# Moving the exponential of a linear-attention feature map from ScalarE to a power operation on GpSimd

## The chip, the cores and the metric

The program runs on one core of one Trainium2 chip. The metric is device time in microseconds (us) of one execution. "Span" is the profiled length of one execution, some 2 to 5 us less than its time. A core has TensorE (PE; PEld is its weight load), VectorE (DVE), ScalarE (ACT), GpSimd (POOL) and SyncE (SP), each with its own in-order instruction queue; semaphores connect them.

## The reference, cut to what matters

Two independent blocks whose outputs stand side by side. A is attention with 32 heads over 2048 tokens. B is attention in four segments of 512 tokens, with a memory between the segments: queries and keys pass through the feature map `phi`, and that is where the change acts.

```python
phi = lambda t: jnp.where(t > 0, t + 1.0, jnp.exp(t))
for s in range(4):
    ...                                  # causal softmax attention inside the segment: a_dot
    pq = phi(qs)
    a_mem = (pq @ M) / (pq @ z + 1e-06)  # what the memory gives (einsums in the original)
    o = g * a_mem + (1.0 - g) * a_dot
    pk = phi(ks)
    M = M + pk.T @ vs
    z = z + pk.sum(over tokens)
```

## The kernel before

The kernel is a Python program that simulates the five engines while it emits instructions. Every operation has a `cost`, the estimate of its time in us, and the order of the instructions in each queue follows from these estimates. On the chip the order is fixed; semaphores only make an engine wait.

```python
class Recorder:
    def op(self, eng, fn, r=(), w=(), cost=0.1, mode="F"):
        ...                              # dependencies from the keys read (r) and written (w)
        t = self.free[eng]
        for d in op.deps:
            t = max(t, d.end + LAT)
        op.end = t + cost                # the plan's idea of when this is done
        self.free[eng] = op.end
        self.all.append(op)              # this order is the engine's queue
```

A group of four heads of one segment is prepared by `b_prep`: 32 groups in all. KQ holds keys and queries of one group, 128 partitions x (2 tiles of 512 columns). The first and the last segment need only one of the two tiles (`nk` is 1), the middle segments both. phi(t) is computed as max(t, 0) + min(exp(t), 1):

```python
    def b_prep(self, n):
        ...
        ex = R.op("ACT", lambda e: e.activation(self.E[:, k0:k1, :], KQ[:, k0:k1, :], ACTF.Exp),
                  r=[("KQB", b, k) for k in range(k0, k1)], w=["E"], cost=0.2 + 0.43 * nk)
        R.op("DVE", lambda e: e.tensor_scalar(PH[:, k0:k1, :], KQ[:, k0:k1, :], 0.0, None, ALU.max), ...)
        yield ("t", ex.end)              # go on when the plan says that the exponential is done
        R.op("DVE", lambda e: e.tensor_scalar(self.E[:, k0:k1, :], self.E[:, k0:k1, :], 1.0, None, ALU.min), ...)
        ph = R.op("DVE", lambda e: e.tensor_tensor(PH[:, k0:k1, :], PH[:, k0:k1, :], self.E[:, k0:k1, :], ALU.add), ...)
        ...                              # memory terms: Mb and Zb on GpSimd, den and amem on VectorE
```

Two other pieces matter. The exponentials of the scores of A and B (`PT<-ps`) are ScalarE's main work. The weighted values of all units gather in a single PSUM bank that VectorE must copy away before TensorE can fill it again:

```python
    def emit_pv(self, u, st, part):
        ...                              # TensorE: values and row sums into the bank OLB
        if end:
            R.op("DVE", lambda e: e.tensor_copy(self.OL[x][:, :], self.ps[:, OLB, :]), r=[("ps", OLB)], w=[("OL", x)], cost=0.66)

    def finish(self, u):                 # VectorE: two reciprocals, then operations with two SBUF inputs
        ...
            R.op("DVE", lambda e: e.scalar_tensor_tensor(L, L, 1.0, rec, ALU.mult, ALU.add, accum_out=...), ...)
            op = R.op("DVE", lambda e: e.tensor_tensor(self.OTA[:, u.g, q0:q0 + QC], O, rec, ALU.mult), ...)
```

In the traces, `OL<-ps` is that copy, `OL<-OL,SQ` and `OTA<-OL,SQ` are the two-input operations of `finish`, and GpSimd's `PT<-PT` (affine select) is the causal mask of B.

Of the kernel before, what the change touches and what calls it, by code (L numbers as in the profile page):

```python
# [6 lines left out]
ACTF = mybir.ActivationFunctionType  # L7
ALU = mybir.AluOpType
AX = mybir.AxisListType
BF, F32 = dt.bfloat16, dt.float32  # L10

P = 128
# [223 lines left out]
class Kernel:  # L236
# [66 lines left out]
    def sb(self, name, shape, dtype=BF):  # L303
        return self.es.enter_context(self.nc.sbuf_tensor(name, shape, dtype))

    def alloc(self):
        sb = self.sb
        self.ps = self.es.enter_context(self.nc.psum_tensor("ps", [P, 8, 512], F32))
        self.psb = self.ps.bitcast(BF)
        self.xA = sb("xA", [P, NI, S])  # L310
        self.OTA = sb("OTA", [P, NG, S])
        self.WoB = sb("WoB", [P, NG, D])
        self.WA = [sb(f"WA{k}", [P, NI, P]) for k in range(3)]
        self.KA = [sb(f"KA{i}", [P, S]) for i in range(2)]
        self.QA = [sb(f"QA{i}", [P, S]) for i in range(2)]
        self.VA = [sb(f"VA{i}", [P, NT, P]) for i in range(2)]
        self.xB = [sb(f"xB{i}", [P, NI, 512]) for i in range(2)]
        self.OTB = [sb(f"OTB{i}", [P, NG, 512]) for i in range(2)]
        self.WB = [sb(f"WB{k}", [P, NI, P]) for k in range(3)]
        self.PT = sb("PT", [P, RING, 512])  # L320
        self.KQB = [sb(f"KQB{i}", [P, 2, 512]) for i in range(2)]
        self.VB = [sb(f"VB{i}", [P, 4, 144]) for i in range(2)]
        self.E = sb("E", [P, 2, 512])
        self.PH = [sb(f"PH{i}", [P, 2, 512]) for i in range(2)]
        self.PKt = sb("PKt", [P, 4, P])
        self.VT = [sb(f"VT{i}", [P, 512]) for i in range(2)]
        self.SQB = [sb(f"SQB{i}", [P, 512]) for i in range(2)]
        self.VTB = self.SQB[1]
        self.SQ = [sb(f"SQ{i}", [P, 512]) for i in range(2)]
        self.Mf = sb("Mf", [P, NG, 129], F32)  # L330
        self.Mb = sb("Mb", [P, P])
        self.Zb = sb("Zb", [P, P])
        self.OL = [sb(f"OL{i}", [P, 2 * QC], F32) for i in range(2)]

        self.rec = [t.bitcast(F32) for t in self.SQ]
        self.rng = self.SQB[0].bitcast(F32)
        self.flag = sb("flag", [P, 2], dt.int32)
        self.den = sb("den", [P, 512], F32)
        self.amem = [sb(f"amem{i}", [P, 512], F32) for i in range(2)]
        self.outsb = [sb(f"outsb{i}", [P, D]) for i in range(2)]  # L340
        self.cbA = [sb(f"cbA{i}", [P, 12], F32) for i in range(2)]
        self.cbB = [sb(f"cbB{i}", [P, 4], F32) for i in range(2)]
        self.beta = sb("beta", [P, 32])
        self.gcol = sb("gcol", [P, 2, 8], F32)
        self.ident = sb("ident", [P, P])
        self.ones32 = sb("ones32", [P, 32])
        self.blk32 = sb("blk32", [P, 32])
        self.ones = sb("ones", [P, P])
        self.diag = [sb(f"diag{i}", [P, P]) for i in range(2)]
        self.maskbd = sb("maskbd", [P, P], F32)  # L350


    def load_WA(self, k, g):
# [72 lines left out]
    def constants(self):  # L426
        R = self.R

        def pool(f, w, r=()):
            R.op("POOL", f, r=r, w=w, cost=0.3)  # L430
        R.op("DVE", lambda e: e.memset(self.PT[:, RING - 1, :], 1.0), w=[("PT", RING - 1)], cost=0.2)
        nb = sum(len(b) for b in SLOTS)
        for b in range(nb):
            R.op("DVE", lambda e, b=b: e.memset(self.ps[:, b, :], 0.0), w=[("ps", b)], cost=0.4)

        R.op("ACT", lambda e: e.activation(self.gcol[:, 0, :], self.PT[:, RING - 1, 0:8], ACTF.Exp), r=[("PT", RING - 1)], w=["gcol"], cost=1.5)
        pool(lambda e: e.memset(self.blk32[:, :], 1.0), ["blk32"])
        pool(lambda e: e.affine_select(self.blk32[:, :], self.blk32[:, :], pattern=[[-32, 4], [0, 8]],
                                       compare_op=ALU.is_ge, fill=0.0, base=0, channel_multiplier=1), ["blk32"])
        pool(lambda e: e.affine_select(self.blk32[:, :], self.blk32[:, :], pattern=[[32, 4], [0, 8]],  # L440
                                       compare_op=ALU.is_ge, fill=0.0, base=31, channel_multiplier=-1), ["blk32"])
        pool(lambda e: e.memset(self.ones[:, :], 1.0), ["ones"])
        pool(lambda e: e.memset(self.ident[:, :], 0.0), ["ident"])
        pool(lambda e: e.affine_select(self.ident[:, :], self.ident[:, :], pattern=[[-1, P]],
                                       compare_op=ALU.not_equal, fill=1.0, base=0, channel_multiplier=1), ["ident"])
        for i in range(2):
            pool(lambda e, i=i: e.memset(self.VB[i][:, :, :], 1.0), [("VB", i)])
        pool(lambda e: e.memset(self.maskbd[:, :], 1.0), ["maskbd"])
        pool(lambda e: e.affine_select(self.maskbd[:, :], self.maskbd[:, :], pattern=[[-32, 4], [0, 32]],
                                       compare_op=ALU.is_ge, fill=0.0, base=0, channel_multiplier=1), ["maskbd"])  # L450
        pool(lambda e: e.affine_select(self.maskbd[:, :], self.maskbd[:, :], pattern=[[32, 4], [0, 32]],
                                       compare_op=ALU.is_ge, fill=0.0, base=31, channel_multiplier=-1), ["maskbd"])
        pool(lambda e: e.memset(self.Mf[:, :, :], 0.0), [("Mf", g) for g in range(NG)])
# [342 lines left out]
    def b_prep(self, n):  # L796
        R = self.R
        s, g = n // 8, n % 8
        b = n % 2
        xb = s % len(self.xB)  # L800
        nxt = n + 1
        KQ, VB, PH = self.KQB[b], self.VB[b], self.PH[b]
# [8 lines left out]
        if self.shifted:  # L811
# [3 lines left out]
            for k in range(2):  # L815
                op = R.op("DVE", lambda e, k=k: e.tensor_tensor(self.SQB[k][:, :], KQ[:, k, :], KQ[:, k, :], ALU.mult),
                          r=[("KQB", b, k)], w=[("SQB", k)], cost=0.36)
# [21 lines left out]
        k0, k1 = (0, 1) if s == 0 else ((1, 2) if s == 3 else (0, 2))  # L839
        nk = k1 - k0  # L840
        if n > 0:
            yield ("ev", ("memB", n - 1))
        yield ("t", R.lastw[("KQB", b, 1)].end)
        ex = R.op("ACT", lambda e: e.activation(self.E[:, k0:k1, :], KQ[:, k0:k1, :], ACTF.Exp),  # L844
                  r=[("KQB", b, k) for k in range(k0, k1)], w=["E"], cost=0.2 + 0.43 * nk)
        R.op("DVE", lambda e: e.tensor_scalar(PH[:, k0:k1, :], KQ[:, k0:k1, :], 0.0, None, ALU.max),
             r=[("KQB", b, k) for k in range(k0, k1)], w=[("PH", b)], cost=0.28 * nk)
        yield ("t", ex.end)
        R.op("DVE", lambda e: e.tensor_scalar(self.E[:, k0:k1, :], self.E[:, k0:k1, :], 1.0, None, ALU.min),
             r=["E"], w=["E"], cost=0.28 * nk)  # L850
        ph = R.op("DVE", lambda e: e.tensor_tensor(PH[:, k0:k1, :], PH[:, k0:k1, :], self.E[:, k0:k1, :], ALU.add),
                  r=["E", ("PH", b)], w=[("PH", b)], cost=0.36 * nk)
        yield ("dve",)
        if s > 0:

            R.op("POOL", lambda e: e.tensor_tensor(self.Mb[:, :], self.Mf[:, g, 0:P], self.maskbd[:, :], ALU.mult),
                 r=[("Mf", g), "maskbd"], w=["Mb"], cost=0.3)
            zb = R.op("POOL", lambda e: e.tensor_scalar(self.Zb[:, :], self.maskbd[:, :], self.Mf[:, g, P:P + 1], None, ALU.mult),
                      r=[("Mf", g), "maskbd"], w=["Zb"], cost=0.3)
# [3 lines left out]
                 r=["Zb", ("PH", b)], w=[("ps", bank)], cost=0.3)  # L863
            op = R.op("DVE", lambda e, bank=bank: e.tensor_scalar(self.den[:, :], self.ps[:, bank, :], 1e-6, None, ALU.add),  # L864
                      r=[("ps", bank)], w=["den"], cost=0.66)
            self.bank_release(bank, op)
            for q in range(4):
# [6 lines left out]
                 r=["Mb", ("PH", b)], w=[("ps", bank)], cost=0.3)  # L874
# [4 lines left out]
                      r=[("ps", bank), "den", "gcol"], w=[("amem", b, 0), ("amem", b, 1)], cost=0.66)  # L879
            self.bank_release(bank, op)  # L880
            self.events.add(("amem", n))
        if s < 3:
# [7 lines left out]
            def fm(e, bank=bank):  # L890
                for tl in range(4):
# [4 lines left out]
                      r=[("ps", bank), ("Mf", g)], w=[("Mf", g)], cost=0.3)  # L896
# [274 lines left out]
```

## Time and profile before

| | before |
|---|---|
| time, median of 3 runs | 1200.93 us (1200.85 to 1205.26) |
| ScalarE, TensorE, VectorE, GpSimd busy | 1125, 1043, 803, 117 us |
| exponentials of phi on ScalarE | 16 x 665 ns and 16 x 1092 ns |

Line numbers (L532) are those of the kernel at hand and shift by a few lines from one kernel to the next. The page of the kernel before: busy time per engine (share of the span, instructions), then the chain of work that ended last by engine and by line.

```profile
PE 1042.5 (87%) x16699; PEld 481.9 (40%) x16927; DVE 803.4 (67%) x1363; ACT 1125.4 (94%) x1256; POOL 116.5 (10%) x192
...
ACT 47%; PE 40%; DVE 10%; issue 3%; DMA 1%; SPq 0%; DVEq 0%
```

ScalarE is nearly always busy, and the chain alternates between it and TensorE. The groups of instructions, by line and shape (count | total us, mean ns | idle time before them):

```profile
L532 ACT ACTIVATE PT<-ps 128x1024 bf16<-128x1024 f32 x1088 | 1012.9, 1061 | 31.5 <-PE ps L506 29.5
...
L844 ACT ACTIVATE E<-KQB 128x1024 bf16<-128x1024 bf16 x16 | 17.5, 1092 | 0.0
...
L844 ACT ACTIVATE E<-KQB 128x512 bf16<-128x512 bf16 x16 | 10.6, 665 | 0.0
```

The second and third line are what the change takes from ScalarE: 17.5 + 10.6 = 28.1 us. The view of tile E says who waits for its result (us in total, times):

```profile
who waited for it (us, times):
  DVE E L849: 2.8, 5
```

VectorE waits for E only 2.8 us in the whole run: the plan places the minimum (line 849) where E is ready.

### The profile page before, as it was taken

To read this page: it belongs to the slowest core of one execution; us is meant where nothing else is said; L and a number is where in the kernel's file an instruction comes from. 1 tells how busy PE (TensorE), PEld (TensorE's weight loads), DVE (VectorE), ACT (ScalarE), POOL (GpSimd) and SP (SyncE) were. 2 spreads that over 40 slices of the span, in tenths; PEclk is the share of its full clock that TensorE was granted. 3 is DMA by queue.
4 is the path that set the end of the run, shared out by engine and by line. 5 is a ranking of instruction groups with operands and counts; after the bars stand their busy time and mean duration, and the time that the engine had idled before them with its cause. 6 is when DMAs were issued, how large, how long until landed. Compare 5 with 4: busy or idle time off the path is not lost.

```text
span 1198.7 us, 37080 instructions
## 1 busy us (share of the span) xinstructions
PE 1042.5 (87%) x16699; PEld 481.9 (40%) x16927; DVE 803.4 (67%) x1363; ACT 1125.4 (94%) x1256; POOL 116.5 (10%) x192
## 2 busy tenths in 40 slices
PE   8998889999888888888988897978989887789996
PEld 4343444444344333334444443434444343334442
DVE  5248567576786687866777768677777668774443
ACT  3799999999999999999999999999999999999990
POOL 1001001010101020200111102010110102010000
PEclk9999999999999979899999998989999898989998
DMA  5461132243111122141212121211221110401101
GB/s 172 100 162 38 32 86 59 60 89 76 42 37 41 39 48 54 31 82 32 68 38 45 46 50 37 60 24 37 49 66 41 32 42 15 102 20 37 37 37 56
DMA packets 198344, 66.45 MB, mean 55 GB/s; under 512 B 189986, under 2 KB 189986, under 8 KB 198178
## 3 DMA queue, kind: packets, MB, share of 16 engines
q1 hardware_dynamic: 198178, 63.99, 23.1%
q8 instruction: 135, 2.21, 0.8%
q14 instruction: 31, 0.25, 0.1%
HBM read 39.85 MB, written 8.39 MB: 40 GB/s over the span
## 4 chain that ended last, share of the span: by engine, by line
ACT 47%; PE 40%; DVE 10%; issue 3%; DMA 1%; SPq 0%; DVEq 0%
ACT PT L532 46%; PE ps L674 21%; PE ps L581 9%; PE ps L506 8%; DVE SQ L604 2%; DVE OL L591 2%; DVE den L870 1%; ACT E L844 1%; DVE OL L608 1%; DVE amem L877 1%; DMA OTA<-in_A_x_dram 1%; DVE OTA L612 0%; DVE den L864 0%; DVE outsb L919 0%; DMA out_dram<-outsb 0%
## 5 line engine op out<-in xcount | busy, mean ns | idle before, releaser
L532 ACT ACTIVATE PT<-ps 128x1024 bf16<-128x1024 f32 (+1 forms) x1216 | 1102.4, 1039 | 32.4 <-PE ps L506 30.1
L581 PE MATMUL ps<-PT,ones 128*32 128x256 bf16 (+1 forms) x4864 | 295.6, 275 | 0.0
L581 PE MATMUL ps<-PT,VA 128*32 128x256 bf16 x4096 | 251.8, 277 | 20.9 <-ACT PT L532 15.0
L506 PE MATMUL ps<-QA,KA 32*128 32x256 bf16 x4096 | 213.2, 277 | 39.6 <-ACT PT L532 31.3
L604 DVE RECIPROCAL SQ<-OL 128x128 f32<-128x128 f32 x256 | 242.8, 948 | 4.9
L674 PE MATMUL ps<-xB,WB 128*128 128x512 bf16 x684 | 179.2, 383 | 21.2 <-issue 11.6
L674 PE MATMUL ps<-xA,WA 128*128 128x512 bf16 x695 | 181.6, 387 | 16.5 <-issue 8.7
L506 PEld LDWEIGHTS ps<-QA,KA 32*128 32x128 bf16 x4096 | 62.7, 92 | 224.8 <-ACT PT L532 201.0
L581 PEld LDWEIGHTS ps<-PT,VA 128*32 128x32 bf16 x4096 | 108.2, 95 | 111.3 <-issue 65.3
L552 POOL TENSOR_SCALAR_AFFINE_SELECT PT<-PT 128x512 bf16<-128x512 bf16 x128 | 85.9, 672 | 666.3 <-ACT PT L532 661.2
L581 PEld LDWEIGHTS ps<-PT,ones 128*32 128x32 bf16 x4864 | 131.6, 98 | 2.5
L591 DVE COPY OL<-ps 128x512 f32<-128x512 f32 x128 | 85.6, 669 | 30.3 <-PE ps L581 29.4
L674 PEld LDWEIGHTS ps<-xA,WA 128*128 128x128 bf16 x768 | 63.2, 99 | 93.9 <-issue 27.9
L674 PEld LDWEIGHTS ps<-xB,WB 128*128 128x128 bf16 x768 | 61.8, 98 | 95.2 <-issue 45.3
L919 DVE CAST outsb<-ps 128x512 bf16<-128x512 f32 x64 | 43.5, 680 | 76.2 <-PE ps L674 71.4
L870 DVE RECIPROCAL den<-den 128x128 f32<-128x128 f32 x96 | 91.2, 950 | 2.3
L684 DVE CAST KQB<-ps 128x512 bf16<-128x512 f32 x64 | 43.7, 683 | 57.8 <-PE ps L674 57.4
L674 PE MATMUL ps<-xA,OTA 128*128 128x512 bf16 x236 | 59.5, 391 | 8.5 <-DVE OTA L612 3.7
L674 PE MATMUL ps<-WoB,OTB 128*128 128x512 bf16 x232 | 59.7, 380 | 6.6 <-issue 2.9
L581 PE MATMUL ps<-PT,VB 128*32 128x256 bf16 (+1 forms) x768 | 50.8, 282 | 15.3 <-DVE OL L591 12.0
L608 DVE SCALAR_TENSOR_TENSOR OL<-OL,SQ 128x256 f32<-128x256 f32 x128 | 58.2, 455 | 2.7
L684 DVE CAST VT<-ps 128x512 bf16<-128x512 f32 x32 | 22.0, 687 | 47.7 <-PE ps L674 44.3
(64 smaller groups left out, 490.9 us busy)
## 6 DMA issues: line engine op xcount, KB each, us to landing
WB<-in_B_wk_dram SPq DMA_DIRECT2D x32, 256.0 KB, 3.0
WB<-in_B_wq_dram SPq DMA_DIRECT2D x32, 256.0 KB, 2.9
WB<-in_B_wv_dram SPq DMA_DIRECT2D x32, 256.0 KB, 3.2
out_dram<-outsb SPq DMA_DIRECT2D x32, 256.0 KB, 2.0
WA<-in_A_wqkv_dram SPq DMA_DIRECT2D x24, 256.0 KB, 3.8
OTA<-in_A_x_dram SPq DMA_DIRECT2D x16, 256.0 KB, 5.6
WoB<-in_B_wo_dram SPq DMA_DIRECT2D x1, 2048.0 KB, 10.2
xA<-in_A_wo_dram SPq DMA_DIRECT2D x1, 2048.0 KB, 10.3
```

Source lines behind the costliest of these rows:

```text
L506: ins = e.matmul(o, l, r, start=True, stop=True)
L532: op = R.op("ACT", lambda e: e.activation(self.PT[:, s0:s0 + n, 0:width], self.ps[:, banks[0]:banks[0] + n, 0:width], ACTF.Exp, bias=cb, s ...
L552: mo = R.op("POOL", lambda e, ap=ap, pat=pat: e.affine_select(ap, ap, pattern=pat, compare_op=ALU.is_ge, fill=0.0, base=0, channel_multipl ...
L581: ins = e.matmul(o, l, r, start=start, stop=end, skip_group_check=True)
L591: R.op("DVE", lambda e: e.tensor_copy(self.OL[x][:, :], self.ps[:, OLB, :]), r=[("ps", OLB)], w=[("OL", x)], cost=0.66)
L604: R.op("DVE", lambda e, cs=cs: e.reciprocal(rec[:, cs], L[:, cs]), r=[ko], w=[k], cost=0.93)
L608: R.op("DVE", lambda e: e.scalar_tensor_tensor(L, L, 1.0, rec, ALU.mult, ALU.add, accum_out=self.rng[:, u.seq:u.seq + 1]), r=[k, ko], w=[k ...
L674: ins = e.matmul(o, l, rh, start=a, stop=z)
L684: op = self.R.op("DVE", lambda e: e.tensor_copy(dst, self.ps[:, bank, :]), r=[("ps", bank)], w=[dkey], cost=0.66)
L844: ex = R.op("ACT", lambda e: e.activation(self.E[:, k0:k1, :], KQ[:, k0:k1, :], ACTF.Exp), r=[("KQB", b, k) for k in range(k0, k1)], w=["E ...
L870: R.op("DVE", lambda e, cs=cs: e.reciprocal(self.den[:, cs], self.den[:, cs]), r=["den"], w=["den"], cost=0.9)
L919: op = R.op("DVE", lambda e, ns=ns, bank=bank, ob=ob: e.tensor_copy(self.outsb[ob][:, ns], self.ps[:, bank, :]), r=[("ps", bank)], w=[("ou ...
```

## The change: its intent, and the diff

ScalarE is the busiest engine and GpSimd the idlest. The exponential of phi is to become `pow(e, t)` on GpSimd, so that ScalarE gets 28 us of its queue back. The plan is told 0.2 + 1.5 us for one tile of 512 columns and 3.2 us for two.

```diff
+        self.base = sb("base", [P, 1], F32)
...
+        pool(lambda e: e.memset(self.base[:, :], 2.718281828459045), ["base"])
...
-        ex = R.op("ACT", lambda e: e.activation(self.E[:, k0:k1, :], KQ[:, k0:k1, :], ACTF.Exp),
-                  r=[("KQB", b, k) for k in range(k0, k1)], w=["E"], cost=0.2 + 0.43 * nk)
+        ex = R.op("POOL", lambda e: e.tensor_tensor(self.E[:, k0:k1, :].rearrange("p k n -> p (k n)"),
+                                                    self.base[:, 0:1].to_broadcast([P, 512 * nk]),
+                                                    KQ[:, k0:k1, :].rearrange("p k n -> p (k n)"), ALU.pow),
+                  r=[("KQB", b, k) for k in range(k0, k1)] + ["base"], w=["E"], cost=0.2 + 1.5 * nk)
```

## The prediction

> **What bounds the kernel now.** The engine table gives ScalarE 1125 us busy of a 1199 us span (94%), TensorE 1043 (87%), VectorE 803 (67%), GpSimd 117 (10%). The chain that ended last is ScalarE for 47%, nearly all of it the score exponentials (1216 instructions, 1102 us), and TensorE for 40%. ScalarE is about 99% busy from 70 to 1050 us, but it is fed by an in-order TensorE queue that is 86 to 90% busy in the same windows.
>
> **What the change removes.** 32 exponentials of phi from ScalarE: 16 of 128x512 (665 ns) and 16 of 128x1024 (1092 ns), 28.1 us in all by the groups of instructions, 2.3% of the span. Since TensorE is near its limit too, I expect half to two thirds of it at most: 12 to 18 us.
>
> **What it adds.** 32 two-input pow operations on GpSimd, of the same sizes. The change's own costs are 1.7 and 3.2 us. From the trace, the ordinary two-input multiply on GpSimd of 128x128 took 407 to 622 ns, so by size alone (an estimate, some 100 ns of it fixed) about 1.3 and 2.5 us for 512 and 1024 columns. The Trainium skill (GPSIMD Engine Reference, section 3.1) says that these operations run as software loops, with about 2.6 cycles per element for a two-input add; no run here shows a pow. A pow in software needs a logarithm and an exponential, so my central guess is three to four times the add: about 5 us for 512 columns and 9 us for 1024.
>
> **How much is on the critical path.** The static schedule of every engine was made with 1.7 and 3.2 us. VectorE's minimum on E stands in its in-order queue at the place where the model had pow finished. Each microsecond that pow is late stops VectorE there (now 2.8 us in all), and behind it the copy of the single PV bank (OL<-ps), which the next PV needs; the ring of probability tiles keeps ScalarE going only for some microseconds. GpSimd's causal masks queue behind pow too. With 5 and 9 us the excess is about 3.3 and 5.8 us; taking about 3 us of slack each time, 16 x 0.5 + 16 x 3 = 56 us, plus some for VectorE operations with two SBUF inputs: the skill (SBUF — State Buffer, who interferes with whom) calls the pair that VectorE and GpSimd share an exclusive lock held for the whole instruction. No run here shows that yet. Less the gain of about 15 us: plus 45 to 50 us.
>
> **Prediction.** 1250 us, 8 in 10 between 1188 and 1550. If pow takes what the change assumes, about 1190 to 1200. Faster by over 2%: 0.05; within 2%: 0.33; slower by over 2%: 0.62.
>
> **What would show each step right or wrong.** ScalarE's busy time must fall by 28 us to about 1097. The group of pow on GpSimd gives its mean by shape: over 4 us for 512 columns is my central case, near 1.7 is the case "same". VectorE's wait at the minimum on E should grow from 2.8 to over 60 us, and TensorE's for OL<-ps and ScalarE's for scores with it. VectorE's two-input operations get longer under a pow if the lock matters.
>
> **What would make it wrong.** Pow being as quick as modelled, or far slower (tens of microseconds each, then 1500 us and more); slack in VectorE's queue larger than 3 us; or the reshuffled greedy schedule winning or losing a per cent by itself.

## The result, and the profile after

The changed kernel takes 4933.02 us (median of 4 runs, 4930.09 to 4938.39) against 1200.89 us before: 4.11 times as long, 95% interval 4.09 to 4.12. Ratios in this document are the mean time of one kernel's fast runs over that of the other's in the same rounds, so they are not quite the ratio of the medians quoted.

The page after, the same lines as above: busy time, then the chain that ended last.

```profile
PE 1109.4 (22%) x16703; PEld 504.3 (10%) x16927; DVE 3083.7 (63%) x1363; ACT 1110.1 (23%) x1224; POOL 4040.5 (82%) x225
...
DVE 45%; POOL 37%; PE 10%; ACT 7%; issue 1%; DMA 0%; SPq 0%; another core or an unknown queue 0%; DVEq 0%
```

ScalarE and TensorE do the same work as before, apart from the 32 exponentials, spread over four times the span. (TensorE's busy time is 67 us higher, at a mean granted clock of 0.61 against 0.97; beside 3732 us this is small, and no run here isolates it.) GpSimd went from 117 to 4041 us. VectorE seems to have 2280 us more work, although it runs the same 1363 instructions; as shown below, most of it is something else than work. GpSimd's groups by shape show where the time starts:

```profile
L846 POOL TENSOR_TENSOR E<-base,KQB 128x1024 bf16<-128x1024 f32 x16 | 2612.1, 163254 | 167.6 <-DVE KQB L686 167.5
L846 POOL TENSOR_TENSOR E<-base,KQB 128x512 bf16<-128x512 f32 x16 | 1311.2, 81950 | 230.2 <-DVE KQB L686 230.2
```

One pow of 512 columns takes 81.95 us, one of 1024 takes 163.25 us; the plan said 1.7 and 3.2, and the prediction 5 and 9. Together the 32 take 3923 us, and the kernel became 3732 us longer.

Three of VectorE's groups in the kernel before (all shapes of a line together; line 846 there is the maximum, line 850 after):

```profile
L608 DVE SCALAR_TENSOR_TENSOR OL<-OL,SQ 128x256 f32<-128x256 f32 x128 | 58.2, 455 | 2.7
...
L612 DVE TENSOR_TENSOR OTA<-OL,SQ 128x256 bf16<-128x256 f32 x64 | 31.5, 492 | 2.2
...
L846 DVE TENSOR_SCALAR PH<-KQB 128x512 bf16<-128x512 bf16 (+1 forms) x32 | 11.5, 360 | 0.0
```

The same three after, and the minimum on E with the idle time before it:

```profile
L850 DVE TENSOR_SCALAR PH<-KQB 128x512 bf16<-128x512 bf16 (+1 forms) x32 | 1432.0, 44749 | 0.0
L610 DVE SCALAR_TENSOR_TENSOR OL<-OL,SQ 128x256 f32<-128x256 f32 x128 | 752.2, 5876 | 2.7
...
L614 DVE TENSOR_TENSOR OTA<-OL,SQ 128x256 bf16<-128x256 f32 x64 | 193.4, 3022 | 2.2
...
L853 DVE TENSOR_SCALAR E<-E 128x512 bf16<-128x512 bf16 (+1 forms) x32 | 18.6, 580 | 1437.7 <-POOL E L846 1437.7
```

So VectorE stood still in two ways: 1438 us waiting for E, and, inside instructions that normally take under half a microsecond, (1432.0 - 11.5) + (752.2 - 58.2) + (193.4 - 31.5) = 2276 us. The two add up to 3714 us, nearly all of the growth of 3732 us. Behind VectorE, everything stands. The timeline of the changed kernel around one pow (start us, duration us):

```profile
1433.36 163.24 POOL L846 TENSOR_TENSOR E<-base,KQB 128x1024 bf16<-128x1024 f32 x1 [0.19 <-DVE KQB L686]
...
1436.39 160.49 DVE L850 TENSOR_SCALAR PH<-KQB 128x1024 bf16<-128x1024 bf16 x1
1596.80 0.67 DVE L593 COPY OL<-ps 128x512 f32<-128x512 f32 x1
...
1597.53 0.40 PE L583 MATMUL ps<-PT,VA 128*32 128x256 bf16 x4 [159.63 <-DVE OL L593]
...
1600.45 1.94 ACT L534 ACTIVATE PT<-ps 128x1024 bf16<-128x1024 f32 x2 [160.45 <-PE ps L508]
```

VectorE's maximum, a 0.4 us instruction, starts 3 us after pow and ends 0.3 us after it. The copy of the PV bank comes next, then TensorE resumes after 160 us, then ScalarE after 160 us.

### The profile page after: what moved, and what is told of

Same layout as the page of the kernel before. It is cut to its first block, busy times and chain, and to the rows that moved or that the text cites. A ratio compares the mean times of both kernels' runs of the same rounds, so it can differ in the third digit from the quotient of the medians.

```text
span 4932.7 us, 37082 instructions
## 1 busy us (share of the span) xinstructions
PE 1109.4 (22%) x16703; PEld 504.3 (10%) x16927; DVE 3083.7 (63%) x1363; ACT 1110.1 (23%) x1224; POOL 4040.5 (82%) x225
## 4 chain that ended last, share of the span: by engine, by line
DVE 45%; POOL 37%; PE 10%; ACT 7%; issue 1%; DMA 0%; SPq 0%; another core or an unknown queue 0%; DVEq 0%
POOL E L846 37%; DVE PH L850 29%; DVE OL L610 9%; ACT PT L534 7%; PE ps L676 5%; DVE OTA L614 3%; PE ps L583 3%; PE ps L508 2%; DVE SQ L606 1%; DVE OL L593 1%; DVE PH L855 0%; DVE E L853 0%; DVE KQB L686 0%; DMA out_dram<-outsb 0%; DVE SQB L686 0%
## 5 line engine op out<-in xcount | busy, mean ns | idle before, releaser
L846 POOL TENSOR_TENSOR E<-base,KQB 128x512 bf16<-128x512 f32 (+1 forms) x32 | 3923.3, 122602 | 397.7 <-DVE KQB L686 397.7
L850 DVE TENSOR_SCALAR PH<-KQB 128x512 bf16<-128x512 bf16 (+1 forms) x32 | 1432.0, 44749 | 0.0
L853 DVE TENSOR_SCALAR E<-E 128x512 bf16<-128x512 bf16 (+1 forms) x32 | 18.6, 580 | 1437.7 <-POOL E L846 1437.7
L610 DVE SCALAR_TENSOR_TENSOR OL<-OL,SQ 128x256 f32<-128x256 f32 x128 | 752.2, 5876 | 2.7
L583 PE MATMUL ps<-PT,VA 128*32 128x256 bf16 x4096 | 270.1, 292 | 870.7 <-DVE OL L593 780.8
L583 PE MATMUL ps<-PT,ones 128*32 128x256 bf16 (+1 forms) x4864 | 318.9, 291 | 0.0
L508 PE MATMUL ps<-QA,KA 32*128 32x256 bf16 x4096 | 223.7, 289 | 262.5 <-DVE PH L855 150.3
L676 PE MATMUL ps<-xA,WA 128*128 128x512 bf16 x696 | 191.9, 405 | 233.3 <-DVE Mf L899 147.6
L614 DVE TENSOR_TENSOR OTA<-OL,SQ 128x256 bf16<-128x256 f32 x64 | 193.4, 3022 | 2.2
L583 PEld LDWEIGHTS ps<-PT,VB 128*32 128x32 bf16 x768 | 22.9, 105 | 1110.1 <-POOL PT L554 396.9
```

What stands on the lines that cost most here:

```text
L508: ins = e.matmul(o, l, r, start=True, stop=True)
L583: ins = e.matmul(o, l, r, start=start, stop=end, skip_group_check=True)
L676: ins = e.matmul(o, l, rh, start=a, stop=z)
L846: ex = R.op("POOL", lambda e: e.tensor_tensor(self.E[:, k0:k1, :].rearrange("p k n -> p (k n)"), self.base[:, 0:1].to_broadcast([P, 512 * ...
```

## The experiments

Theory 1: pow itself is slow on GpSimd, per column, whatever it is given; everything else follows from that. Theory 1 leaves open how a slow pow stops the other engines: through those who wait for its result (theory D, dependency), or by keeping VectorE out of SBUF ports that, by this theory, both share (theory L, lock). The rival to theory 1: a producer of E on GpSimd is costly by its place, whatever the operation.

### 1. Pow by itself: m1_bench

The kernel before with a row of GpSimd instructions after all its work, each waiting for the one before (core of the edit; `b2` is 2.0 in place of e, `W` holds ones):

```diff
+        pool(lambda e: e.tensor_tensor(X[:, 0:512], be(P, 512), K[:, 0:512], ALU.mult))
+        pool(lambda e: e.tensor_tensor(X[:, 0:1024], be(P, 1024), K[:, 0:1024], ALU.mult))
+        pool(lambda e: e.tensor_tensor(X[:, 0:128], be(P, 128), K[:, 0:128], ALU.pow))
+        pool(lambda e: e.tensor_tensor(X[0:16, 0:127], be(16, 127), K[0:16, 0:127], ALU.pow))
+        pool(lambda e: e.tensor_tensor(X[0:1, 0:122], be(1, 122), K[0:1, 0:122], ALU.pow))
+        pool(lambda e: e.tensor_tensor(X[:, 0:126], b2(P, 126), K[:, 0:126], ALU.pow))
+        pool(lambda e: e.tensor_tensor(X[:, 0:125], be(P, 125), W[:, 0:125], ALU.pow))
+        pool(lambda e: e.tensor_tensor(X[:, 0:64], be(P, 64), K[:, 0:64], ALU.pow))
```

> The kernel before, and after all its work a row of GpSimd instructions that nobody but the next one waits for, each timed by the profile. Theory 1 (the software of pow itself is slow, per element): multiply 128x512 about 1.3 us and 128x1024 about 2.5 us, pow 128x128 about 21 us (0.65 us + 128 x 0.159 us, from the trace after), base 2 in place of e and exponents of 1.0 in place of data the same 0.159 us per column. Rival (pow is slow only for this data or this base): the variants with base 2 or exponent 1.0 differ by a factor. If the software goes lane by lane, one partition takes a small part of what 16 take; if it works on all lanes at once, 1, 16 and 128 partitions take the same per column.

Measured, timeline of GpSimd at the end of that run, in the order of the edit:

```profile
1194.89 1.04 POOL L657 TENSOR_TENSOR E<-base,KQB 128x512 bf16<-128x512 f32 x1 [129.81 <-DVE E L653]
1196.01 1.89 POOL L658 TENSOR_TENSOR E<-base,KQB 128x1024 bf16<-128x1024 f32 x1
1197.98 20.75 POOL L659 TENSOR_TENSOR E<-base,KQB 128x128 bf16<-128x128 f32 x1
1218.81 20.56 POOL L660 TENSOR_TENSOR E<-base,KQB 16x127 bf16<-16x127 f32 x1
1239.45 19.76 POOL L661 TENSOR_TENSOR E<-base,KQB 1x122 bf16<-1x122 f32 x1
1259.29 20.41 POOL L662 TENSOR_TENSOR E<-base,KQB 128x126 bf16<-128x126 f32 x1
1279.77 20.25 POOL L663 TENSOR_TENSOR E<-base,ones 128x125 bf16<-128x125 f32 x1
1300.10 10.52 POOL L664 TENSOR_TENSOR E<-base,KQB 128x64 bf16<-128x64 f32 x1
```

A multiply costs (1.89 - 1.04) / 512 = 1.7 ns per column, a pow (20.75 - 10.52) / 64 = 160 ns: some 95 times as much. All pow lines give 162 to 164 ns when divided by their columns: base 2 or e, data or ones, 128 partitions, 16 or one. So the cost belongs to the operation and its number of columns, it was the same for both bases and for both kinds of exponent tried, and using fewer partitions saved nothing. Exponents of other sizes were not tried: the keys here are close to 0 (the reference's inputs give them a standard deviation of about 0.0025, an estimate: 32 x 0.05 x 0.05 / 32). The Trainium skill (Perfetto Trace Analysis, section GPSIMD Engine Instruction) advises to time GpSimd by the spacing of starts and not by the reported duration; here both agree (1197.98 to 1218.81 is 20.83 us). The run itself, a single one whose state is unknown, took 1318.62 us, which is its added tail. Why a pow takes this long, no run shows.

### 2. The same change with multiply: m2_mult

```diff
-                                                    KQ[:, k0:k1, :].rearrange("p k n -> p (k n)"), ALU.pow),
+                                                    KQ[:, k0:k1, :].rearrange("p k n -> p (k n)"), ALU.mult),
```

> The changed kernel with multiply in place of pow, everything else the same (wrong result on purpose). Theory 1 (pow's own duration is the whole loss): 1185 to 1205 us, ScalarE busy about 1097 us, GpSimd about 60 us more than before. Rival (a producer of E on GpSimd is costly by its place: handover, in-order queue, the pair of ports shared with VectorE): 1250 us or more.

Measured: 1187.78 us against 1202.87, ratio 0.987 (0.985 to 0.989), the result wrong as intended. The page's busy line:

```profile
PE 1037.5 (87%) x16703; PEld 486.6 (41%) x16927; DVE 801.2 (68%) x1363; ACT 1101.7 (93%) x1224; POOL 161.2 (14%) x225
```

The rival falls. With an operation as quick as the plan believes, the move is worth 15 us, and VectorE no longer waits for E at all. This is the whole prize of the idea.

### 3. Pow as long as the prediction had assumed: m3_dose

Pow acts on 28 columns, or on 27 of each of two tiles; the rest of E keeps the constant 1 from the start.

```diff
+        pool(lambda e: e.memset(self.E[:, :, :], 1.0), ["E"])
...
+        nc = 28 if nk == 1 else 27
+        ex = R.op("POOL", lambda e: e.tensor_tensor(self.E[:, k0:k1, 0:nc],
+                                                    self.base[:, 0:1].unsqueeze(1).to_broadcast([P, nk, nc]),
+                                                    KQ[:, k0:k1, 0:nc], ALU.pow),
```

> The changed kernel with pow on only 28 columns (one 512-column tile) or 2 x 27 columns (two tiles), so that pow takes about 5.1 and 9.2 us, the durations that the prediction assumed; the rest of E keeps a constant (wrong result on purpose). The prediction's model of the critical path (3 us slack, excess counts): 1250 us. Rival, every microsecond of pow stops VectorE and with it everything: up to 1190 + 229 = about 1420 us. Rival, the queues absorb it: 1210 us or less.

Measured: 1240.46 us against 1202.87, ratio 1.030 (1.028 to 1.032). Pow took 4.82 and 8.99 us on average. The view of tile E:

```profile
who waited for it (us, times):
  DVE E L855: 50.7, 18
```

Against m2_mult the run is 52.7 us longer, and VectorE's wait for E, absent in m2_mult, is 50.7 us. So the prediction's model of the critical path was sound: it said 56 us for pows of 5 and 9 us (the same sum gives 47 us for 4.82 and 8.99), and "everything stops for all of every pow" or "the queues absorb it" would have missed. The result passed the comparison with the reference although most of E was the constant 1: the arguments of phi are so small in this input (about 0.0025, the estimate above) that exp(t) is nearly 1. A passed comparison is therefore weak evidence about this exponential here.

### 4. A pow that nobody waits for: m4_lone, then n1_lone512 and n2_lone576

Does pow stop VectorE without being waited for? In the trace of the changed kernel, long VectorE instructions occur under pows of 1024 columns alone, never under those of 512. First try, with one pow of 512 columns at the end of B:

```diff
+                    if u.kn == 31 and u.half == 0 and k == len(todo):
+                        R.op("POOL", lambda e: e.tensor_tensor(self.E[:, 0, :], self.base[:, 0:1].to_broadcast([P, 512]),
+                                                               self.KQB[1][:, 1, :], ALU.pow),
+                             r=[("KQB", 1, 1), "base"], w=["E"], cost=0.1)
```

> The kernel before, with one pow of 128x512 (about 82 us) on GpSimd after its last causal mask, writing E when nobody reads it any more. Theory D (the loss comes only through engines that wait for E or for GpSimd's queue): unchanged, 1200 +- 3 us. Theory L (VectorE instructions with two SBUF inputs or in a fast mode can't run while GpSimd holds the shared ports): VectorE stands still in one instruction for most of 82 us while attention of A still goes on, and the time is 1265 to 1283 us.

Measured: 1281.33 us against 1202.87, ratio 1.065. It looks like theory L, but the run was badly made: the condition held twice, and a mask came between the two pows. GpSimd's timeline:

```profile
1064.16 81.95 POOL L560 TENSOR_TENSOR E<-base,KQB 128x512 bf16<-128x512 f32 x1
1146.08 0.65 POOL L554 TENSOR_SCALAR_AFFINE_SELECT PT<-PT 128x512 bf16<-128x512 bf16 x1
```

TensorE waited 77.8 us for that mask, so the run shows only the cost of a mask queued behind a pow in GpSimd's in-order queue. The second try puts exactly one pow behind the very last mask, once with 512 and once with 576 columns:

```diff
+                    if u.kn == 31 and it.scored + n == len(it.slots) and k == n:
+                        flat = lambda t: t[:, :, :].rearrange("p k n -> p (k n)")[:, 0:576]
+                        R.op("POOL", lambda e: e.tensor_tensor(flat(self.E), self.base[:, 0:1].to_broadcast([P, 576]),
+                                                               flat(self.KQB[1]), ALU.pow),
+                             r=[("KQB", 1, 0), ("KQB", 1, 1), "base"], w=["E"], cost=0.1)
```

> The kernel before with exactly one pow of 128x512 (82 us) on GpSimd behind the very last causal mask; nobody reads what it writes. The trace after showed that VectorE instructions with two tensor inputs or in a fast mode were held up only under pows of 1024 columns. Theory D (a pow costs only through those who wait for its result or its queue): 1202 +- 4 us. Theory L (any pow holds the shared ports all the time): 1265 us or more.

> The same with 576 columns (about 92 us). If a pow of more than 512 columns is worked off in pieces of 512 and keeps VectorE's two-input instructions out until its last input is read, VectorE stands for about 75 us in one instruction under it and the time is 1265 to 1285 us. If the length alone counts and nobody waits: 1202 +- 4 us, as with 512.

Measured: with 512 columns 1201.42 us against 1200.54, ratio 1.000 (0.998 to 1.002); with 576 columns 1284.52 us, ratio 1.069 (1.067 to 1.072). The timelines of GpSimd and VectorE under these two pows, first with 512 columns:

```profile
1064.94 82.22 POOL L561 TENSOR_TENSOR E<-base,KQB 128x512 bf16<-128x512 f32 x1
...
1065.39 1.14 DVE L638 SCALAR_TENSOR_TENSOR OL<-OL,gcol,SQ 128x256 f32<-128x256 f32 x1
1066.56 0.42 DVE L640 TENSOR_TENSOR OTB<-OL,amem 128x256 bf16<-128x256 f32 x1
```

and with 576 columns:

```profile
1066.78 92.48 POOL L561 TENSOR_TENSOR E<-base,KQB 128x576 bf16<-128x576 f32 x1
...
1067.23 81.70 DVE L638 SCALAR_TENSOR_TENSOR OL<-OL,gcol,SQ 128x256 f32<-128x256 f32 x1
```

An 82 us pow of 512 columns held a two-input VectorE instruction for some 0.7 us at its start and then let VectorE work freely; it cost nothing. A pow only 10 us longer held the same instruction until 82.2 us after the pow's start, the time that 512 columns take, and cost 84 us. So a pow of more than 512 columns can stop VectorE though nobody waits for it.

The trace of the changed kernel shows two kinds of hold-up under its 16 pows of 1024 columns. All 11 of the `OL<-OL,SQ` and `OTA<-OL,SQ` instructions (two inputs in SBUF) that started in the first half of such a pow ended 82.6 to 82.7 us after the pow's start. The single-input maximum (line 850, 0.43 us for 1024 columns in the kernel before) fell under 13 of these pows, and ended each time 0.3 us after the pow's end, whether it had started in the first half or the second. Reciprocals and copies out of PSUM kept their usual length. Under pows of 512 columns the maximum ran as usual.

The Trainium skill (SBUF — State Buffer, section Who interferes with whom) says that a VectorE instruction with two SBUF inputs contends with a GpSimd instruction that reads SBUF, and that one in a 2-port performance mode contends with GpSimd, the first to issue having the shared pair for the whole instruction. The contention is here; for two-input instructions neither run shows a hold for the whole of the pow. That the input is read piece by piece and the two-input instructions are released when the last piece is read is my reading of these times, not something a record names. It does not say why the maximum stands longer; that stays open.

### 5. Does that hold-up cost time in the changed kernel: n3_split

Every pow of 1024 columns becomes two of 512; nothing else changes.

```diff
-        ex = R.op("POOL", lambda e: e.tensor_tensor(self.E[:, k0:k1, :].rearrange("p k n -> p (k n)"),
-        ...
+        for k in range(k0, k1):
+            ex = R.op("POOL", lambda e, k=k: e.tensor_tensor(self.E[:, k, :], self.base[:, 0:1].to_broadcast([P, 512]),
+                                                             KQ[:, k, :], ALU.pow),
+                      r=[("KQB", b, k), "base"], w=[("E", k)], cost=0.1 + 1.5)
```

> The changed kernel with each pow of 1024 columns as two pows of 512, so that VectorE is not held up in the ports any more (if the trace after was read rightly). Theory D (VectorE, in order, would stand at the minimum on E just as long): 4930 us within 1%, with VectorE's wait at that minimum up from 1438 to about 3700 us and its 75 to 160 us long instructions gone. Theory L (the port hold-up costs time of its own): under 4700 us.

Measured: 4868.02 us. Against the changed kernel's 4933.02 us (from another chip job, each beside its own runs of the kernel before: 4.054 and 4.106 times) that is 1.3% less. The page's busy line, and the list of waits:

```profile
PE 1091.5 (22%) x16703; PEld 499.6 (10%) x16927; DVE 808.7 (17%) x1363; ACT 1108.3 (23%) x1224; POOL 4048.4 (83%) x241
...
DVE E L853 <- POOL E L847: 3651.0, 32, 159.6
```

VectorE's blown-up busy time is gone, 3084 to 809 us (under these pows the maximum of 1024 columns took 0.42 us in the median), and its wait for E rose from 1438 to 3651 us. The time hardly moved. Theory D holds: the port hold-up was real, but it only changed in which instruction VectorE stood. At most the last 1.3% (the expectation said within 1%) belongs to the hold-up and to the different plan of this run; the runs don't part these two.

### 6. A plan that knows what pow takes: n4_truecost and p1_planned

The first takes n3_split with `cost=82.0` for a tile. The second takes m3_dose with `cost=0.9 + 4.15 * nk` (5.05 and 9.2 us) in place of 1.7 and 3.2.

> As the run before it, but the schedule is told what a pow really takes (82 us for 512 columns in place of 1.6). GpSimd's own work is about 3925 + 117 us, so nothing under about 4040 us is to be had. If the loss above that is the schedule's wrong idea of pow: 4050 to 4250 us, with ScalarE's work under the pows. If each pow is in a chain that can't be overlapped anyway: over 4700 us.

Measured (two runs): 4420.93 us, ratio 3.68. This lies between the two expectations. ScalarE's other work did move under the pows (the chain that ended last is 90% GpSimd), so some 450 us of the loss was the plan's wrong idea. Of the 380 us above the 4040 us of GpSimd's own work, GpSimd spent 325 us waiting for the next group's keys and queries:

```profile
POOL E L847 <- DVE KQB L686: 324.5, 23, 64.4
```

> As the run with 28 and 2 x 27 columns (4.8 and 9.0 us a pow, 1240 us), but the schedule is told 5.05 and 9.2 us in place of 1.7 and 3.2. If its 52 us over the multiply version come from VectorE standing at E earlier than the data is there, a true plan takes them away: 1185 to 1200 us, with VectorE's wait for E near zero. If a longer producer costs by itself (longer chain per head group, masks queued behind it): 1215 us or more.

Measured: 1190.69 us against 1202.34, ratio 0.990 (0.989 to 0.992). The view of tile E:

```profile
who waited for it (us, times):
  POOL E L848: 4.0, 2
  DVE E L855: 1.8, 2
```

The same instructions of 4.8 and 9 us that cost 52.7 us with a wrong plan cost 2.9 us (1190.69 - 1187.78, from two jobs) with a right one. In this statically ordered kernel an error in the cost number was a cost by itself.

### 7. A real exponential of cheap GpSimd instructions: q1_squares and q2_squares2

If about 9 us per group are free, an exponential of additions and multiplications might win. The formula (1/2 + v*v/512)^16 with v = max(t + 16, 0) is an approximation (its relative error is 0.07% at -1 and 5% at -4), so this is a trial of the time and not a general replacement. Core of the edit against the kernel before, as in the second run:

```diff
+        D, kd = self.amem[b][:, :], [("amem", b, 0), ("amem", b, 1)]     # q1: D = self.den, key "den"
+        for k in range(k0, k1):
+            R.op("POOL", lambda e, k=k: e.tensor_scalar(D, KQ[:, k, :], 16.0, 0.0, ALU.add, ALU.max), ..., cost=2.05)
+            R.op("POOL", lambda e: e.tensor_tensor(D, D, D, ALU.mult), ..., cost=1.14)
+            R.op("POOL", lambda e: e.tensor_scalar(D, D, 1.0 / 512, 0.5, ALU.mult, ALU.add), ..., cost=0.72)
+            for _ in range(3):
+                R.op("POOL", lambda e: e.tensor_tensor(D, D, D, ALU.mult), ..., cost=1.14)
+            ex = R.op("POOL", lambda e, k=k: e.tensor_tensor(self.E[:, k, :], D, D, ALU.mult), ..., cost=1.14)
```

> The kernel before with the exponential of phi on GpSimd as seven additions and multiplications in float32, (1/2 + v*v/512)^16 with v = max(x + 16, 0), which is exp(x) within 0.07% at -1 and 5% at -4, and is told to the schedule as 1.1 to 1.2 us an instruction (about 8.2 us a tile, 16.4 for two). If a producer of E on GpSimd costs nothing as long as the plan knows its duration: 1186 to 1196 us. If the seven instructions really take longer than planned, or their float32 tile (shared with the memory's denominators) makes new waits: 1200 us or more.

Measured: 1287.32 us, ratio 1.071. The seven instructions of a tile took 7.9 us together, where 8.2 were planned (the first of them 1.95 in place of 1.1), but the float32 scratch was also the tile of the memory's denominators, and GpSimd waited for its last reader:

```profile
POOL den L846 <- DVE amem L884: 284.7, 14, 24.5
```

> As the run before it, with the float32 scratch in the buffer that the same head group's memory term fills later (free at that time) in place of the denominators' tile, whose last reader GpSimd had to wait for (285 us in all), and with the measured durations in the plan (2.05, 1.14 and 0.72 us an instruction, 8.5 us a tile). If that wait was the loss: 1186 to 1198 us and GpSimd's wait for the memory term gone. If a chain of 8 to 17 us per head group on GpSimd is by itself too long: 1215 us or more.

Measured: 1213.85 us against 1202.73, ratio 1.009 (1.008 to 1.011). That wait is gone, and the run lies between both expectations. ScalarE is down to 1103 us busy, but VectorE is up from 803 to 844 us. Its operation `OL<-OL,SQ` is longer on average, against 455 ns before:

```profile
L608 DVE SCALAR_TENSOR_TENSOR OL<-OL,SQ 128x256 f32<-128x256 f32 x128 | 69.2, 540 | 2.5
```

So the idea does not beat the kernel before in this form. How much of the missing 23 us against p1_planned is contention, and how much is the chain of up to 17 us per group, stays open.

One thing could not be tried: pow on VectorE in place of GpSimd. This is a compiler's answer and no run: the changed kernel with VectorE named for the instruction in place of GpSimd is refused, while the same with multiply for pow compiles.

## Why the prediction was wrong

- The failed step, as the prediction put it: "my central guess is three to four times the add: about 5 us for 512 columns and 9 us for 1024". It measured 81.95 and 163.25 us, 16 and 18 times that guess and 79 and 86 times the multiply of the same size (1.04 and 1.89 us). This one term of the sum is the miss. The reason given for it, that a pow needs a logarithm and an exponential, was not tested: no run shows how pow is worked out, and why it takes 160 ns a column stays open. The prediction named "far slower (tens of microseconds each, then 1500 us and more)" as a danger, yet its range ended at 1550.
- The scaling by size was not the miss: for the ordinary operation it gave 1.3 and 2.5 us, and 1.04 and 1.89 were measured, so it was too high by a quarter to a third.
- What the move is worth: predicted 12 to 18 us, measured 15.1 us with multiply in pow's place (1202.87 - 1187.78). ScalarE's busy time fell by 23.7 us there and not by 28, since neighbouring ScalarE instructions overlap a little (the score exponentials sum to 1109 us by shape but fill 1102 us together); in the changed kernel it fell by 15 us.
- The critical path: predicted 56 us for pows of 5 and 9 us, less the gain. With pows of 4.8 and 9.0 us the chip gave 52.7 us over the multiply version and 1240 us in all, against the prediction's 1250. With the true durations in the same arithmetic (an estimate: 16 x (81.95 - 1.7 - 3) + 16 x (163.25 - 3.2 - 3), less 15 us) the sum is 3734 us; measured were 3732. That the two agree to 2 us is luck: the 3 us of slack were a guess, and splitting the pows alone moved the time by 65 us. What is shown is that nearly every microsecond of excess stopped the kernel.
- VectorE's wait at the minimum on E was predicted to grow to over 60 us; it did, to 1438 us, and to 3651 us once the pows were split. The rest of VectorE's standstill hid as busy time.
- Longer two-input VectorE operations under a pow were predicted "if the lock matters". They came, up to 82.4 us (the instructions of 160 us are the single-input maximum), but only under pows of more than 512 columns, and splitting those pows moved the time by just 1.3%.

## What to carry to other kernels

Before work is moved to an idle engine, time the very operation there, in one short run: a neighbour that looks alike (multiply) was some 80 times quicker, and no factor of three covers that. In a kernel with a fixed order like this one, an instruction that is late against its plan stops its consumer's whole in-order queue, and a plan that was 3 to 6 us too short for each of 32 instructions cost more than the move could win, while the same instruction rightly planned was nearly free. When an engine's busy time grows without new work, look for instructions far above their usual duration: they are waits in disguise, and removing such a wait does not help if the next instruction would have waited for the same thing.

## What the Trainium skill lacked or had wrong

- GPSIMD Engine Reference, section 3 (Performance versus the Vector engine): it describes elementwise work on GpSimd as about 2 times slower than VectorE and gives no cost for pow. The runs show 160 ns per column (81.95 us for 128x512), some 95 times the multiply's 1.7 ns per column, and the same with base 2, with exponents of 1.0, and on 16 partitions or one.
- The same section gives about 2.6 cycles per element for a two-input `tensor_tensor`, which at that page's 1.2 GHz is 2.2 ns (an estimate from the page's two figures); the multiply here (bfloat16 data, a broadcast float32 operand) took 1.7 ns per column between 512 and 1024 columns.
- SBUF — State Buffer, section Who interferes with whom: the hold for the whole instruction is stated for the 2-port performance modes, and no time is given for a VectorE instruction with two SBUF inputs. With a pow of 512 columns such an instruction ended 1.6 us into the 82 us pow; with 576 columns it was held for 81.7 us, beside a pow of 92.5 us; with 1024 columns, until 82.6 us of 163. The section does not make the hold depend on the length of the GpSimd instruction, as it did here between 512 and 576 columns.
